# Quarter-block products of seven for the last two blocks' output matmul, with weight combinations made on GpSimd

## The chip, the cores and the metric

The kernel runs on one core of a Trainium2 chip. The metric is device time in microseconds (us) of one execution, the median of several. TensorE (PE in the profile, PEld its weight loads), VectorE (DVE), ScalarE (ACT), GpSimd (POOL) and SyncE (SP, which issues the DMAs here) run side by side and wait for one another through semaphores.

## The reference

Linear attention with exponential features feeds a feed-forward layer. There are 8 batches of 576 tokens with 8 heads of 64; side by side, the heads give 4608 tokens of 512 features.

```
phi(x) = concat(exp(p - m), exp(-(p - m)))     with p = x @ w_phi (64x128), m = max |p| of a token and head
kv = phi(k)^T v ; z = sum of phi(k) ; x = (phi(q) kv) / (phi(q) z + 1e-6)
h = x @ w_in                                   (4608x512 @ 512x2048)
g = h * erf(softplus(h))
out = g @ w_out                                (4608x2048 @ 2048x512), float32
```

## The kernel before

The feed-forward part works in nine blocks of 512 tokens (s = 0 to 8; blocks 0 to 7 are the first 512 tokens of each batch, block 8 the last 64 of all eight). A block's h is made in four units u of 512 features, each held as two tiles h of 128 x 1024. Numbers are split into two float16 parts, a rounded one and a remainder, and a product is three matmuls: high by high, high by low, low by high. Every matmul is issued as a pair, each of which fills 64 of the 128 output rows (`mm`).

x @ w_in is already made by seven products of quarter blocks instead of eight (the forms A11, S3, A12, S2, S1, S4, A22 of x against B11, T3, B21, T2, T1, B22, T4 of w_in; S and T are sums and differences of quarters). `split` makes the float16 parts of a form of x, which a DMA then transposes, and `combine` makes the sums; `split_weights` does both for w_in. For a unit, `h_unit` yields the seven products; `snap` (ACT) and `add` (DVE) take them out of the PSUM banks into h. `erf_gate` then runs softplus and erf on ACT and the multiplication by h on DVE, and splits g into `gh` (ACT) and `gl` (DVE).

g @ w_out is made plainly, by `o_piece`: for a half round (s, r, t), with r the half of the features and t the half of the tokens, four pieces of 12 matmul pairs of 512 columns. After r = 0 the sum goes to DRAM as a partial sum (`parts`), after r = 1 it is fetched, added to and stored.

The attention of the next batch runs between these on the same engines (`project`, `front`, `kv_piece`, `n_piece`, `t_piece`); it is done by about 760 us. The weights are loaded, unpacked and split between 18 and 258 us of the run.

The order of the work is set by a planner in the kernel (`Plan.run`). Every operation is recorded with an engine, an assumed cost, a priority and its buffers; the planner simulates the five engines with these costs and issues the operations in the order that it finds. So constants such as `STAY`, `SLACK` (how much later than planned an operand of TensorE is taken to be ready), `GATE_OFF` (priority offsets of the gate), the numbers of buffers and ranges such as `X_POOL` or `XC_POOL` (blocks whose work goes to POOL) move instructions on all engines. Operations marked `port=True` are assumed to exclude each other between DVE and POOL. Where TensorE would wait for over 600 ns by the plan, the planner issues filler matmuls on the tile `hot`, in pairs.

In `split_weights` four subtractions for each weight tile are recorded as work of POOL, but issued when `eng` already names DVE again:

```
    pool = u < T_POOL
    eng = nc.gpsimd if pool else nc.vector
    tt = lambda o, oc, x, xc, y, yc, r: op(POOL if pool else DVE, 750 if pool else 330, lambda: eng.tensor_tensor(...), ...)
    ...
    for f, x, c, key in (...):
        pool = u in LI_POOL and f in LF_POOL
        eng = nc.gpsimd if pool else nc.vector
```

## Time and profile before

| | us |
|---|---|
| median of 3 runs | 968.59 (968.54 to 968.77) |
| the profiled execution | 968.28 |
| its span, first to last instruction | 966.5 |
| TensorE busy | 947.7 |
| DVE busy | 752.7 |
| ACT busy | 681.9 |
| POOL busy | 43.9 |

Busy times are sums over the span and say little about a stage; the prediction reads them stage by stage. A row of a group gives the line of the kernel, the engine, the operation, the tiles written and read, and then count and durations; "idle before" is the time in which the engine waited, with what ended the wait. Matmul durations overlap, so their pace is read from the starts.

### The profile page before, as it was taken

Reading aid. Unit: us, or ns where it says so; the run is one execution under the profiler, and the core shown is the slowest. Engines: PE = TensorE matmul, PEld = TensorE weight load, DVE = VectorE, ACT = ScalarE, POOL = GpSimd, SP = SyncE. Lnnn points to the kernel's source line nnn. Section 1 sums busy time; section 2 is a strip of 40 time slices with the busy share of each in tenths; the row PEclk is TensorE's granted clock in tenths of the full one; section 3 lists DMA queues with packets and bytes.
Section 4 is the critical chain, followed back from the end, with each engine's and each line's share of the span. In section 5 each row is a group of like instructions: output and inputs, shape, how many; then the busy total and the mean of one; then the engine's idle time right before and its main releaser. Section 6 shows DMA issues by size and latency. Waiting matters only on the chain.

```text
span 966.5 us, 35295 instructions
## 1 busy us (share of the span) xinstructions
PE 947.7 (98%) x15806; PEld 754.5 (78%) x15806; DVE 752.7 (78%) x1351; ACT 681.9 (71%) x1000; POOL 43.9 (5%) x35
## 2 busy tenths in 40 slices
PE   9989989899999999999999999999999999999998
PEld 7878867768777878788787878787878787887875
DVE  6999999999977896898888886889896754335442
ACT  7877888777877576957687766766666755657571
POOL 0021100131310000000000000000000000000000
PEclk9999999999999999999999999999999999999999
DMA  9489999699855766386948493596735863342112
GB/s 330 113 217 307 271 283 289 240 324 304 175 164 159 186 123 205 84 212 148 224 120 196 127 221 101 142 223 166 164 69 148 219 153 132 110 144 89 56 56 77
DMA packets 173336, 170.82 MB, mean 177 GB/s; under 512 B 124544, under 2 KB 125696, under 8 KB 173184
## 3 DMA queue, kind: packets, MB, share of 16 engines
q1 hardware_dynamic: 173184, 168.57, 64.9%
q8 instruction: 123, 2.02, 0.9%
q14 instruction: 29, 0.24, 0.1%
HBM read 110.07 MB, written 29.10 MB: 144 GB/s over the span
## 4 chain that ended last, share of the span: by engine, by line
PE 78%; DVE 3%; issue 0%; DVEq 0%
PE bank L424 65%; PE bank L434 9%; PE bank L633 4%; DVE gl L1034 0%; DVE m L581 0%; DVE half L482 0%; DVE big L530 0%; DVE big L592 0%; DVE half L480 0%; DVE big L964 0%; DVE half L520 0%; DVE big L1030 0%; DVE uq L592 0%; DVE big L754 0%; DVE half L478 0%
## 5 line engine op out<-in xcount | busy, mean ns | idle before, releaser
L424 PE MATMUL bank<-half,big 128*64 128x256 f16 x4536 | 274.1, 273 | 3.4 <-DVE big L964 2.3
L424 PEld LDWEIGHTS <-big 128*64 128x64 f16 x4536 | 247.7, 110 | 22.8 <-issue 4.5
L442 ACT ACTIVATE big<-bank 128x512 f32<-128x512 f32 x190 | 111.1, 603 | 143.7 <-PE bank L424 140.5
L424 PE MATMUL bank<-woh,gh 128*64 128x512 f16 x1024 | 199.1, 380 | 2.3 <-ACT gh L1033 2.3
L424 PE MATMUL bank<-woh,gl 128*64 128x512 f16 x1024 | 198.6, 380 | 1.2 <-DVE gl L1034 1.2
L424 PE MATMUL bank<-wol,gh 128*64 128x512 f16 x1024 | 198.9, 379 | 0.0
L442 ACT ACTIVATE big<-big 128x512 f32<-128x512 f32 x206 | 127.6, 628 | 71.0 <-DVE big L592 35.0
L424 PEld LDWEIGHTS <-gh 128*64 128x64 f16 x2048 | 119.2, 110 | 74.7 <-ACT gh L1033 2.9
L964 DVE SCALAR_TENSOR_TENSOR big<-bank,big 128x512 f32<-128x512 f32 x108 | 73.9, 686 | 71.6 <-PE bank L424 67.0
L1030 DVE TENSOR_TENSOR big<-big,big 128x1024 f32<-128x1024 f32 x72 | 86.2, 1221 | 32.5 <-ACT big L1026 32.4
L581 DVE TENSOR_REDUCE m<-bank 128x4 f32<-128x512 f32 x144 | 92.7, 684 | 21.7 <-PE bank L633 21.5
L424 PEld LDWEIGHTS <-gl 128*64 128x64 f16 x1024 | 61.3, 110 | 45.9 <-DVE gl L1034 1.7
L424 PE MATMUL bank<-half,wi 128*64 128x256 f16 x1512 | 93.3, 273 | 1.2 <-DVE big L964 0.7
L1034 DVE TENSOR_TENSOR gl<-big,gh 128x1024 f16<-128x1024 f32 x64 | 80.4, 1265 | 13.5 <-ACT gh L1033 13.5
L424 PEld LDWEIGHTS <-wi 128*64 128x64 f16 x1512 | 81.4, 110 | 6.3 <-issue 1.9
L434 PE MATMUL bank<-kv,big 128*64 128x65 f32 x2304 | 84.6, 222 | 0.0
L434 PEld LDWEIGHTS bank<-v,big 128*64 128x64 f32 x2016 | 77.2, 137 | 8.0 <-ACT big L442 0.9
L434 PE MATMUL bank<-v,big 128*64 128x65 f32 (+1 forms) x2016 | 82.1, 228 | 0.3 <-ACT big L442 0.3
L434 PEld LDWEIGHTS bank<-kv,big 128*64 128x64 f32 x2304 | 78.6, 138 | 4.2 <-issue 0.2
L1010 ACT ACTIVATE big<-big 128x1024 f32<-128x1024 f32 x72 | 72.6, 1050 | 0.8 <-DVE big L964 0.4
L1033 ACT CAST gh<-big 128x1024 f16<-128x1024 f32 x64 | 65.5, 1039 | 4.0 <-DVE big L1030 3.9
L592 DVE TENSOR_TENSOR uq<-bank,m 128x512 f32<-128x512 f32 x72 | 49.2, 683 | 0.6 <-PE bank L664 0.5
(69 smaller groups left out, 1127.3 us busy)
## 6 DMA issues: line engine op xcount, KB each, us to landing
big<-wd SPq DMA_DIRECT2D x81, 512.0 KB, 5.0
ld<-in_qk_dram SPq DMA_DIRECT2D x31, 576.0 KB, 4.8
part<-half SPq DMA_DIRECT2D x36, 256.0 KB, 3.5
half<-part SPq DMA_DIRECT2D x36, 256.0 KB, 3.3
v<-in_vp_dram SPq DMA_DIRECT2D x28, 325.0 KB, 4.0
big<-in_moe_w_in_dram SPq DMA_DIRECT2D x32, 256.0 KB, 5.3
big<-in_moe_w_out_dram SPq DMA_DIRECT2D x16, 512.0 KB, 5.8
out_dram<-half SPq DMA_DIRECT2D x32, 256.0 KB, 2.3
```

The costliest lines, as they stand in the source:

```text
L424: nc.tensor.matmul(o[half], a[:, half], b, start=start, stop=stop, **kw)
L434: nc.tensor.matmul(o[half], a[:, half], b, start=first and c == 0, stop=last and c == 1)
L442: nc.scalar.activation(out_(), in_(), func, **k)
L581: op(DVE, 600, lambda: nc.vector.tensor_reduce(m.t, ps(), axis=AX.X, op=ALU.max, apply_absolute_value=True), r=[b], w=[m])
L592: op(DVE, 600, lambda: nc.vector.tensor_tensor(to(), ps(), m.t.unsqueeze(2).to_broadcast([P, GT, NF]), op=ALU.subtract), r=[b, m], w=[key])
L633: nc.tensor.matmul(both[nm].t[:, t * P : (t + 1) * P], x()[rows], w.t[rows, :], start=i == 0, stop=i == len(terms) - 1)
L964: op(DVE, 640, lambda: nc.vector.scalar_tensor_tensor(h.t[:, c * 512 : c * 512 + 512], b.t, HSCALE, h.t[:, c * 512 : c * 512 + 512], op0=A ...
L1010: fn = lambda: nc.scalar.activation(L.t, h.t, AF.Softplus, scale=1.0 / SG)
L1030: op(DVE, 1140, lambda h=h, L=L: nc.vector.tensor_tensor(h.t, h.t, L.t, op=ALU.mult), r=[L, h], w=[h], port=True, off=GATE_OFF[0] * (v + 1))
L1033: op(ACT, 940, lambda h=h, a=a: nc.scalar.copy(halfs(a), h.t), r=[h], w=[a], off=GATE_OFF[1] * (v + 1))
L1034: op(DVE, 1140, lambda h=h, a=a, b=b: nc.vector.tensor_tensor(halfs(b), h.t, halfs(a), op=ALU.subtract), r=[h, a], w=[b], port=True, off=G ...
```

## The change

For blocks 7 and 8 (`OW = 7`) g @ w_out is made by seven products too. `g_forms` takes the place of the two splits in `erf_gate`: for each unit four combinations of quarters of g on DVE, and seven splits, each a copy on ACT and a subtraction on DVE. `t_forms`, called once in each of the eight steps from step 16 on, makes the combinations of w_out on POOL out of the float16 parts held in `woh` and `wol`, splits them (ACT and POOL) and stores them to DRAM (`td`). `o_chunk` takes the place of `o_piece`: for each half of the features (r) 14 chunks of 12 matmul pairs of 256 columns, with the forms of g as weights and the forms of w_out as moving operand, and an addition in SBUF (`oc`) after each product instead of the partial sums in DRAM.

The diff changes more. The subtractions of `split_weights` now keep their engine (`eng=eng`), so they are issued on POOL. The remainders of x are made on POOL for all blocks and not for the first three alone, and the combinations of x on POOL for blocks 0 and 1. Seven copies of kv go from DVE to ACT, eight remainders of `halve` from POOL to DVE, and three more groups of keys take their maximum as a bias on ACT. Buffers that had sets of their own now share the 36 of `half`, and a dozen planner constants have other values.

```
-STAY2 = 9000.0
-N1 = 9
+STAY2 = 5000.0
+N1 = 5
-X_POOL = 0, 3
+X_POOL = (0, 9)
-XC_POOL = 0, 0
-HL_POOL = 8, 16
+XC_POOL = (0, 2)
+HL_POOL = (8, 12)
-HALF = 22
+HALF = 36
+N2 = 28
-W_EARLY = 4
+W_EARLY = 3
-BIASED = (0, 18)
-KV_ACT = (0, 0)
+BIASED = (0, 21)
+KV_ACT = (1, 8)
-GATE_OFF = (6000.0, 7000.0, 9000.0)
-W_FROM = 14
-W_EACH = 7
+GATE_OFF = (5000.0, 5500.0, 6500.0)
+W_FROM = 18
+W_EACH = 5
-STAY = 1500.0
+STAY = 4000.0
-SLACK = 2000.0
+SLACK = 1000.0
+OW = 7
+TW_FROM = 16
+TW_STEP = 1
+TW_POOL = 1
+T_AHEAD = 9000.0
...
-        tt = lambda o, oc, x, xc, y, yc, r: op(POOL if pool else DVE, 750 if pool else 330, lambda: eng.tensor_tensor(...
+        tt = lambda o, oc, x, xc, y, yc, r, eng=eng: op(POOL if pool else DVE, 640 if pool else 335, lambda: eng.tensor_tensor(...
...
+        if n[0] >= OW:
+            h0, h1 = hs.pop((n, 0)), hs.pop((n, 1))
+            for v, h in ((0, h0), (1, h1)):
+                L = pair[v]
+                op(DVE, 1140, lambda h=h, L=L: nc.vector.tensor_tensor(h.t, h.t, L.t, op=ALU.mult), ...)
+            g_forms(n, h0, h1, pair[0])
+            return
...
+    def g_forms(n, h0, h1, L):
...
+        def split_g(f, src, key):
+            g = gf[n, f] = buf("gf")
+            hv = lambda i: halfs(g)[:, i * 512 : i * 512 + 512]
+            act(520, lambda: hv(0), src, AF.Copy, [key], [(g, 0)], off=at[0])
+            op(DVE, 600, lambda: nc.vector.tensor_tensor(hv(1), src(), hv(0), op=ALU.subtract), ...)
...
+        split_g(A11, piece(h0, 0), (h0, 0))
+        mix_g(piece(L, 0), piece(h0, 0), piece(h1, 0), True, ...)
+        split_g(S3, piece(L, 0), L)
...
+    def t_forms(r, j):
...
+        for F in (4 * r + j, 8 + 4 * r + j):
+            want(("o", F))
+            f = buf("wf")
+            op(POOL_, k, lambda f=f, F=F: eng.tensor_tensor(f.t, woh.t[:, F, :], wol.t[:, F, :], op=ALU.add), ...)
...
+                act(310, lambda i=i, hv=hv: hv(i, 0), lambda x=x, c=c: x.t[:, c], AF.Copy, ...)
+                op(POOL_, k // 2 + 40, lambda ...: eng.tensor_tensor(hv(i, 1), x.t[:, c], hv(i, 0), op=ALU.subtract), ...)
+                op(SP, 430, lambda ...: nc.sync.dma_start(d.t[:, j * Q : j * Q + Q], o.t[:, i * Q : i * Q + Q]), ...)
...
+    def o_chunk(o, i):
...
+            for k in range(2):
+                for z, (gl_, wl_) in enumerate(((0, 0), (0, 1), (1, 0))):
+                    mm(109, lambda ...: (
+                        bank.t[:, k * Q : k * Q + Q], halfs(g)[:, gl_ * 512 + q * Q + k * P : ... + P], w(wl_)), ...)
...
+        if (s, key) not in outs:
+            c = outs[s, key] = buf("oc")
+            op(DVE, 600, lambda: nc.vector.tensor_scalar_mul(c.t, bank.t, scale), r=[bank], w=[c])
+        else:
+            c = outs[s, key]
+            op(DVE, 640, lambda: nc.vector.scalar_tensor_tensor(c.t, bank.t, scale, c.t, op0=ALU.mult, op1=ALU.add), ...)
...
+        plan.slack = SLACK if N2 > n > N0 else SLACK0
```

Two places show how the order moves. The first is the split of the first weight tiles of w_in, early in the program. DVE before: L520 are the subtractions in question, L480 and L482 unpack a weight tile, L530 makes its remainders, L581 and L592 belong to the attention.

```order
L520 TENSOR_TENSOR half11_153<-half0_142 128x256
L754 TENSOR_TENSOR big9_85<-bank3_64,dn0_195 128x4x64
L480 SCALAR_TENSOR_TENSOR half10_152<-big13_89,half10_152 128x512
L530 SCALAR_TENSOR_TENSOR wi00_73<-half0_142,wi00_73 128x256
L482 SCALAR_TENSOR_TENSOR half10_152<-big13_89,half10_152 128x512
L530 SCALAR_TENSOR_TENSOR wi00_73<-half11_153,wi00_73 128x256
L520 TENSOR_TENSOR half11_153<-half10_152,half0_142 128x256
L581 TENSOR_REDUCE m0_177<-bank4_65 128x4
L581 TENSOR_REDUCE m1_178<-bank1_62 128x4
L520 TENSOR_TENSOR half12_154<-half10_152,half11_153 128x256
```

DVE in the changed kernel at the same place (L505 was L482, L553 was L530, L607 was L581):

```order
L780 TENSOR_TENSOR big9_85<-bank3_64,dn0_203 128x4x64
L553 SCALAR_TENSOR_TENSOR wi00_73<-half12_162,wi00_73 128x256
L553 SCALAR_TENSOR_TENSOR wi00_73<-half15_165,wi00_73 128x256
L553 SCALAR_TENSOR_TENSOR wi00_73<-half17_167,wi00_73 128x256
L607 TENSOR_REDUCE m0_191<-bank4_65 128x4
L607 TENSOR_REDUCE m1_192<-bank1_62 128x4
```

And POOL in the changed kernel, where the four subtractions (L543) now stand, followed by a combination of x (L841) and remainders of x (L814):

```order
L543 TENSOR_TENSOR half17_167<-half12_162 128x256
L543 TENSOR_TENSOR half17_167<-half15_165,half12_162 128x256
L543 TENSOR_TENSOR half18_168<-half15_165,half17_167 128x256
L543 TENSOR_TENSOR half18_168<-half15_165,half18_168 128x256
L841 TENSOR_TENSOR half21_171<-big9_85 128x512
L814 TENSOR_TENSOR half22_172<-big9_85,half22_172 128x2x256
```

The four subtractions of a tile, eight times over, have left DVE, and POOL has them ahead of the forms of x.

The second place is the end of the program, after the last unit's softplus. ACT before, from the last erf on:

```order
L1026 ACT_TABLE_LOAD
L1026 ACTIVATE big9_85<-big9_85 128x1024
L1023 ACTIVATE big0_76<-big0_76 128x1024
L1024 ACT_TABLE_LOAD
L1033 CAST half11_153<-big5_81 128x1024
L1033 CAST half10_152<-big10_86 128x1024
```

ACT in the changed kernel from there on; the third copy behind the table load is the form A11 of the last unit, and the copies from big3 and big17 belong to the unit before:

```order
L1052 ACT_TABLE_LOAD
L1052 ACTIVATE big4_80<-big4_80 128x1024
L1049 ACTIVATE big8_84<-big8_84 128x1024
L1050 ACT_TABLE_LOAD
L465 ACTIVATE half28_178<-big3_79 128x512
L465 ACTIVATE half6_156<-big17_93 128x512
L465 ACTIVATE half0_150<-big1_77 128x512
L465 ACTIVATE half8_158<-big4_80 128x512
L465 ACTIVATE half1_151<-big1_77 128x512
```

TensorE in the changed kernel around the first use of that form (half0_150); the rows left out are the rest of the same 24 matmuls, of the 18 fillers, and of the next 24:

```order
L447 LDWEIGHTS half7_157
L447 MATMUL bank0_61<-woh0_74,half7_157 64x256
...
L1331 LDWEIGHTS hot_205
L1331 MATMUL bank2_63<-hot_205 64x512
...
L447 LDWEIGHTS half0_150
L447 MATMUL bank6_67<-woh0_74,half0_150 64x256
```

The two wide casts have become nine narrow copies, and 18 fillers stand ahead of the last unit's first out-product, where the order before had none. Between the last product of h and these fillers stand 152 matmuls of 256 columns. In the whole program the fillers number 98 instead of 90, and 14 of either stand at the very start.

167 lines of the change are left out of this document (138 added, 29 removed).

## The prediction

> **What bounds the kernel now.** I read the page's head, then a table of stretches, then the rows behind the stretches that differ.
>
> ```profile
> span 966.5 us, 35295 instructions
> PE 947.7 (98%) x15806; PEld 754.5 (78%) x15806; DVE 752.7 (78%) x1351; ACT 681.9 (71%) x1000; POOL 43.9 (5%) x35
> ```
>
> ```profile
> core 0: us, PE busy (x) PEld busy (x) DVE busy (x) ACT busy (x) POOL busy (x), PEclk, DMA share, GB/s
> 0.00:20.00 20.00, 18.55 (x290) 14.57 (x291) 11.99 (x25) 13.62 (x45) 0.70 (x6) 1.00 0.90 318
> 20.00:94.00 74.00, 69.45 (x1410) 59.72 (x1406) 72.87 (x190) 59.35 (x177) 10.47 (x9) 1.00 0.79 226
> 94.00:203.00 109.00, 101.05 (x1729) 82.69 (x1726) 107.02 (x213) 89.94 (x139) 19.11 (x12) 1.00 0.92 271
> 203.00:240.00 37.00, 37.00 (x624) 28.69 (x624) 36.58 (x62) 29.78 (x39) 2.56 (x2) 1.00 1.08 308
> 240.00:480.00 240.00, 240.00 (x4158) 186.79 (x4156) 204.22 (x346) 173.50 (x226) 11.09 (x7) 1.00 0.69 170
> 480.00:764.00 284.00, 283.62 (x5048) 224.79 (x5045) 231.75 (x417) 197.30 (x253) 0.00 (x0) 1.00 0.64 158
> 764.00:936.00 172.00, 172.00 (x2336) 140.57 (x2335) 79.19 (x94) 109.52 (x118) 0.00 (x0) 1.00 0.37 110
> 936.00:966.50 30.50, 26.05 (x242) 16.71 (x238) 9.13 (x11) 8.91 (x9) 0.00 (x0) 0.97 0.25 69
> ```
>
> Three stages. Up to 203 us DVE is the limit: it works 72.9 of 74 and 107.0 of 109 us, and TensorE is idle 1.45 + 4.55 + 7.95 = 13.95 us. From 203 us to the last matmul TensorE never pauses but for 0.38 us, at full clock, so there each microsecond of matmul taken away comes off the end. In the last stretch TensorE stops 4.45 us before the end, for the last addition and its store. Filler matmuls on the tile hot hide more idle time; after the first 14 they are 76, all before 90 us, in pairs as the ordinary ones:
>
> ```profile
> L1178 PE MATMUL bank<-hot x90: 376/379/636, 1.4 to 89.1; 128*64 128x512 f16 x90
> ```
>
> **The change, part by part.** *Fewer matmuls.* The pace stands in the rows of TensorE near the end, where the starts tell more than the modelled ends:
>
> ```profile
> 930.96 0.41 PE L424 MATMUL bank<-wol,half 128*64 128x512 f16 x2
> 931.17 0.63 PE L424 MATMUL bank<-woh,half 128*64 128x512 f16 x4
> 931.61 0.41 PE L424 MATMUL bank<-wol,half 128*64 128x512 f16 x2
> 931.82 0.63 PE L424 MATMUL bank<-woh,half 128*64 128x512 f16 x4
> 932.25 0.41 PE L424 MATMUL bank<-wol,half 128*64 128x512 f16 x2
> 932.47 0.63 PE L424 MATMUL bank<-woh,half 128*64 128x512 f16 x4
> 932.90 2.81 PE L424 MATMUL bank<-half,big 128*64 128x256 f16 x48
> 935.52 0.41 PE L424 MATMUL bank<-wol,half 128*64 128x512 f16 x2
> ```
>
> Three pairs of 512 columns start 0.648 us apart (930.96 to 931.61), 0.216 a pair; 24 pairs of 256 columns take 2.62 us (932.90 to 935.52), 0.109 a pair. Two blocks hold 2 x 16 x 12 = 384 pairs of 512 in o_piece, 82.9 us. Instead o_chunk makes 2 x 2 x 14 x 12 = 672 pairs of 256, 73.2 us. That is 9.7 us less, all in the stage where TensorE never waits. A pair of 256 columns loads as many weights as one of 512; the 0.109 us comes from h products that load at that rate too, so it already holds the loads.
>
> A rule of the Trainium skill speaks against this: TensorE: Matmul & The Clock Gate, section "Back-to-back issue gap", puts a stream of weight load and matmul at about 81 ns for 128 columns and 131 ns for 512, so that halving the columns saves far less than half. Interpolated, an estimate from that page, 256 columns would cost three quarters of 512. The trace disagrees: 0.109 is half of 0.216.
>
> *The start.* The diff also takes work from DVE before 240 us. In before the 32 subtractions of split_weights, meant for POOL, were issued on DVE (the name eng is bound again before they are issued); now they are on POOL. The 8 combinations of x of blocks 0 and 1 go to POOL too, 7 copies of kv and 3 subtractions to ACT, while 8 remainders of halve come back from POOL.
>
> ```profile
> L520 DVE TENSOR_TENSOR half<-half,half x24: 397/419/1118, 27.5 to 188.6; 128x256 f32<-128x256 f32 x24
> L520 DVE TENSOR_TENSOR half<-half x8: 396/421/425, 25.0 to 184.5; 128x256 f32<-128x256 f32 x8
> L1034 DVE TENSOR_TENSOR gl<-big,gh x12: 1209/1218/2175, 126.6 to 252.7; 128x1024 f16<-128x1024 f32 x12
> 186.16 1.01 DVE big L530 x3
> 187.50 1.20 DVE m L581 x2
> 192.34 5.37 POOL L788 TENSOR_TENSOR half<-big,half 128x512 f16<-128x512 f32 x1 [18.89 <-issue]
> 197.66 1.16 POOL L788 TENSOR_TENSOR half<-half,half 128x512 f16<-128x512 f32 x1
> 51.58 0.72 DVE L520 TENSOR_TENSOR half<-half,half 128x256 f32<-128x256 f32 x1
> 285.23 2.24 DVE L1034 TENSOR_TENSOR gl<-big,gh 128x1024 f16<-128x1024 f32 x1
> 228.15 0.66 DVE L964 SCALAR_TENSOR_TENSOR big<-bank,big 128x512 f32<-128x512 f32 x1
> ```
>
> On a full DVE an operation of 256 columns costs 0.33 us (1.01 for three), one of 512 costs 0.60. So the 32 subtractions are 10.6 us, the 8 combinations 4.8, kv copies some 2.3, the three subtractions 1.6: 19.3 us off. Back come 8 halves of halve, 5.4 in all, half of it this early. Counting the DVE rows of both orders up to the 18th addition of a product's bank (the one at 228.15 us) at these prices gives 207.7 us before and 194.6 after: 13.1 less, since some attention moves ahead too. That is the gain's upper end, close to the 13.95 us that TensorE idles. The lower end: POOL and DVE disturb each other. One POOL subtraction took 5.37 us instead of 1.16, and DVE operations that normally take 0.42 and 1.22 have maxima of 1.12 and 2.17. Thirteen DVE rows, the first at 51.58 us and the last at 285.23, stand 10.2 us above their medians, 0.35 for each of the 29 tensor operations of POOL up to then. Up to the last weight split POOL now has some 33 operations more, mostly short: up to 11.6 us given back, so a gain of 1.5; and none if TensorE then waits elsewhere. The order still holds 66 fillers after the first 14, against 76. I take the middle between 0 and 13.1, 6 us, since both prices are measured and the net lies between.
>
> By the Trainium skill (Perfetto Trace Analysis, section "Optimizing Scalar/DVE Operations") the two engines share a read port of SBUF, so that moving work between them might not help; by that this term is 0. The stretched rows agree that there is a conflict, not that it eats all.
>
> *The tail.* After the last product the old order has out-product pieces of earlier units to run. The new one has 76 pairs of 256, 8.3 us, then 9 filler pairs, then the first piece that needs the last unit. The latency comes from these rows:
>
> ```profile
> 935.06 1.28 ACT L1010 ACT_TABLE_LOAD   x1
> 936.35 2.00 ACT L1010 ACTIVATE big<-big 128x1024 f32<-128x1024 f32 x2
> 938.37 1.28 ACT L1026 ACT_TABLE_LOAD   x1
> 939.67 1.06 ACT L1026 ACTIVATE big<-big 128x1024 f32<-128x1024 f32 x1
> 940.63 1.04 ACT L1023 ACTIVATE big<-big 128x1024 f32<-128x1024 f32 x1
> 941.69 1.28 ACT L1024 ACT_TABLE_LOAD   x1
> 940.75 2.36 DVE L1030 TENSOR_TENSOR big<-big,big 128x1024 f32<-128x1024 f32 x2 [3.71 <-ACT big L1026]
> 943.03 0.69 DVE L1066 TENSOR_SCALAR half<-bank 128x512 f32<-128x512 f32 x1
> 962.08 0.69 DVE L1073 SCALAR_TENSOR_TENSOR half<-bank,half 128x512 f32<-128x512 f32 x1 [4.49 <-PE bank L424]
> ```
>
> Counted from the product's end (935.52), the last table load ends 7.45 us later. ACT then copies three quarters at about 0.6, the third being the one needed (9.25), and DVE subtracts (0.69): 9.9 us against 8.3 of cover. The fillers stretch this to 8.3 + 9 x 0.216 = 10.2, so the loss is 1.9 us. What follows is ready about as it is used. The last addition and store (4.45 us) stay.
>
> *What costs nothing.* Each of 8 units gets 7 splits and 4 combinations of 0.6 on DVE for two subtractions of 1.2: 4.2 us more, 34 in all, with 12 more additions 41; DVE works only 79 of 172 us from 764 on. ACT gets some 2 us more a unit, on 110 of 172. POOL's 80 forms of w_out and 42 remainders of x for blocks 3 to 8 lie behind 240 us; there DVE is busy 436 of 524 us, loses 42 x 0.6 = 25, and may be held 122 x 0.35 = 43. The stores and loads of the forms (4 and 8 MB), less 4 MB of partial sums, fall where the DMA share is 0.25 to 0.69. If this cover goes, TensorE waits at the first product of a block (below).
>
> *Order.* The planner's margin for TensorE (SLACK) falls from 2000 to 1000 ns, and to 600 from step 28. The trace shows no wait at the lower margin. It can gain no more than the 0.38 us idle after 203; at worst I allow 4, a third of what TensorE idles in the DVE-bound stage. I take 1, nearer to the full rows from 240 on.
>
> Sum: -9.7 - 6 + 1.9 + 1 = -12.8. The profiled execution took 968.28 us (span 966.5 and 1.8 around it), 0.3 below the median of 968.59: 955.5 against it, 956 as a median.
>
> **The rivals.** (a) The start gives nothing, because POOL holds DVE up for as long as it relieves it, and small waits come: -9.7 + 1.9 + 1 to 4 = 961.5 to 964.5. The 5.37 us row speaks for it; the short operations speak against. (b) The start gives all: -9.7 - 13.1 + 1.9 = 947.5. DVE's 98% up to 203 speaks for it; 66 fillers in the order against.
> (c) Slower: x remainders on POOL come late at the starts of blocks 3 to 8. SP issues in order, so a transpose waiting for POOL holds back the weight fetches behind it, and TensorE waits for either. Price: 5.37 - 1.16 = 4.2 us a block, six blocks 25 us: 968.3 - 12.8 + 25 = 981. It decides from the fourth late block on (12.8 / 4.2 = 3). Against it: blocks 0 to 2 had their remainders on POOL in the busiest stage, and no wait of TensorE there was put down to a transposed x. (d) The pieces of 256 columns cost three quarters of a 512: 672 x 0.162 = 108.9, 26 more than now, about 991 with the other terms (-6 + 1.9 + 1). The eight rows at 931 speak against it.
>
> **How the numbers follow.** My forecast, start term 2 to 11: 0.62. (a) 0.14, (b) 0.15, (c) 0.05, (d) 0.01; 0.03 for terms that cancel. A measurement here tells 0.2% (1.9 us). (a) and (b) are both faster, so faster 0.91, same 0.03, slower 0.06. The range leaves out the slow cases and the edges of (a) and (b): 948 to 964.
>
> **What would show it.** Right: matmuls of 256 columns on woh 0.109 a pair in blocks 7 and 8; 32 operations of L543 on POOL; TensorE idle before 203 us down from 13.95 to 6 to 10; 18 filler matmuls ending some 14 us before TensorE's end with no wait behind them over 0.3 us. Wrong: TensorE waiting between 240 and 764 us for a transposed x or for POOL, DVE rows stretched by more than 0.35 us for each POOL operation, or a hole at the tail well over 2 us.

## The result, and the profile after

The changed kernel takes 974.48 us (median of 4 runs, 973.05 to 976.77), the kernel before in the same comparison 968.68 (968.54 to 969.30): a ratio of 1.0062 (1.005 to 1.0074), 5.8 us slower. Forecast were 956.0 and 948 to 964. The profiled execution took 973.05 us, 4.8 more than that of before and the shortest of its four. The head of its page:

```profile
span 971.0 us, 36924 instructions
PE 944.2 (97%) x16390; PEld 783.3 (81%) x16390; DVE 801.7 (83%) x1354; ACT 713.1 (73%) x1097; POOL 210.0 (22%) x189
```

POOL works 210.0 us instead of 43.9, DVE 801.7 instead of 752.7, and TensorE is busy 3.5 us less. The table of stretches shows where TensorE's pauses are now (columns as in the prediction's table: the stretch, its length, busy time and count of PE, PEld, DVE, ACT and POOL, then the granted clock of TensorE, the DMA share and GB/s):

```profile
0.00:20.00 20.00, 18.55 (x296) 14.48 (x296) 11.90 (x25) 14.07 (x47) 0.70 (x6) 1.00 0.91 327
20.00:94.00 74.00, 69.10 (x1362) 58.16 (x1361) 72.76 (x173) 61.16 (x182) 29.97 (x30) 1.00 0.80 230
94.00:203.00 109.00, 103.39 (x1766) 83.43 (x1764) 107.64 (x190) 90.44 (x158) 32.54 (x26) 1.00 0.95 283
...
240.00:480.00 240.00, 233.97 (x4056) 186.88 (x4054) 208.36 (x319) 178.64 (x250) 101.00 (x96) 0.99 0.70 176
480.00:764.00 284.00, 282.59 (x5026) 226.31 (x5024) 229.82 (x394) 199.20 (x254) 33.79 (x24) 1.00 0.64 158
764.00:836.00 72.00, 69.68 (x918) 56.11 (x916) 40.59 (x53) 40.89 (x48) 9.45 (x7) 0.98 0.67 176
```

TensorE's idle time in a stretch is its length less PE's busy time. Up to 203 us it is 1.45 + 4.90 + 5.61 = 11.96 us, 2.0 less than before. From 203 to 836 us, where it was 0.38, it is now 6.03 + 1.41 + 2.32 = 9.76. The reader should also see two clocks that stood at 1.00 before: 0.99 and 0.98.

The rows of TensorE that carry most of the new pauses, the row behind one of them, and the pause of the tail; the bracket gives the wait and what ended it:

```profile
348.46 0.85 PE L659 MATMUL bank<-w,ld 64*128 64x128 f16 x24 [2.00 <-DVE big L780]
...
643.02 0.85 PE L659 MATMUL bank<-w,ld 64*128 64x128 f16 x24 [1.07 <-DVE big L618]
...
772.17 2.16 PE L447 MATMUL bank<-half,big 128*64 128x256 f16 x24 [2.32 <-DVE big L990]
774.06 1.55 PE L447 MATMUL bank<-woh,half 128*64 128x512 f16 x6
...
954.40 2.81 PE L447 MATMUL bank<-big,half 128*64 128x256 f16 x48 [0.46 <-DVE half L1171]
```

All of these waits are for DVE (of those over 1 us after 203 us one more, 1.10 at 277.71, is put down to ACT). At 348.46 and 643.02 the matmuls waiting are those of a projection (L659), at 772.17 those of a product of h. The last row is the pause of the tail. Two of the waits cost twice, as windows laid behind them show:

```profile
349.60:353.00 3.40, 3.40 (x30) 2.36 (x26) 3.30 (x7) 2.28 (x5) 0.00 (x0) 0.50 0.50 154
...
772.90:776.30 3.40, 3.40 (x27) 2.46 (x24) 2.38 (x4) 0.00 (x0) 0.00 (x0) 0.50 0.00 0
```

For 3.4 us after the wait of 2.00 and again after that of 2.32 the granted clock is 0.50. The 24 matmuls at 772.17 take 1.89 us from start to start of the next group (772.17 to 774.06), where 24 like them take 1.31 us in the tail rows below. Each of these windows costs some 1.7 us, half of its length.

What held DVE up ahead of 348.46 stands in its rows:

```profile
338.75 3.21 DVE L704 COPY half<-half 128x1024 uint16<-128x1024 uint16 x2
...
344.69 0.75 DVE L707 COPY big<-half 128x1024 uint16<-128x1024 uint16 x1 [2.13 <-DMA half<-half]
```

The copies of L704 prepare a transpose by DMA, and those of L707 take its result. The median of an L704 is 0.69 us; these two took 3.21 while POOL made combinations of w_out (L1111, 338.24 to 341.41). Then DVE stood 2.13 us until the transposed tile had landed, and the L780 that TensorE waited for came behind that.

And what held DVE up ahead of 772.17, with POOL's row in that time:

```profile
768.06 0.43 DVE L811 CAST half<-big 128x512 f16<-128x512 f32 x1 [2.35 <-DMA big<-tails]
768.40 0.68 DVE L841 TENSOR_TENSOR half<-big 128x512 f32<-128x512 f32 x1
769.00 2.18 DVE L1067 TENSOR_TENSOR half<-big,half 128x1024 f16<-128x1024 f32 x1
...
771.44 0.68 DVE L990 SCALAR_TENSOR_TENSOR big<-bank,big 128x512 f32<-128x512 f32 x1
...
768.62 1.48 POOL L814 TENSOR_TENSOR half<-big,half 128x512 f16<-128x512 f32 x1 [7.18 <-DVE half L811]
```

DVE works in the order of its rows. It waited 2.35 us for a load (tile tails), then made one of its subtractions (L1067) in 2.18 us, whose median over the run is 1.22, while POOL made a remainder of x (from 768.62 to 770.10). The addition that TensorE waited for (L990, 0.68 us) stood behind both. No form of w_out is in this, only the order and a remainder of x on POOL.

POOL's groups show what its operations really take (count, then busy time and mean ns of one):

```profile
L814 POOL TENSOR_TENSOR half<-big,half 128x512 f16<-128x512 f32 x54 | 79.0, 1470 | 426.8 <-DVE half L811 346.4 <-issue 46.1 <-ACT half L809 22.1
L1126 POOL TENSOR_TENSOR half<-half,half 128x256 f16<-128x256 f32 x32 | 25.6, 826 | 22.8 <-ACT half L465 22.8
L1116 POOL TENSOR_TENSOR half<-half,half 128x256 f32<-128x256 f32 x24 | 23.4, 985 | 0.6
L543 POOL TENSOR_TENSOR half<-half,half 128x256 f32<-128x256 f32 x24 | 22.8, 962 | 15.9 <-DVE half L505 13.1 <-DVE dn L766 2.2
L1111 POOL TENSOR_TENSOR half<-woh,wol 128x512 f32<-128x512 f16 x16 | 22.2, 1407 | 29.1 <-DVE half L704 29.1
```

The planner had been told 1160 ns for L814 and L1111, and 620 to 640 for L1116, L1126 and L543. Means are 1470, 1407, 985, 826 and 962. The rows of t_forms (L1111, L1116, L1126) lie at 220 to 388 us: their priority comes from steps 16 to 23, 500 us and later, but POOL was free, so the planner placed them far earlier. POOL is at work 101.0 of the 240 us between 240 and 480.

### The profile page after: what moved, and what is told of

It is laid out like the page before. It is cut to its first block, busy times and chain, and to the rows that moved or that the text cites. A ratio compares the mean times of both kernels' runs of the same rounds, so it can differ in the third digit from the quotient of the medians.

```text
span 971.0 us, 36924 instructions
## 1 busy us (share of the span) xinstructions
PE 944.2 (97%) x16390; PEld 783.3 (81%) x16390; DVE 801.7 (83%) x1354; ACT 713.1 (73%) x1097; POOL 210.0 (22%) x189
## 4 chain that ended last, share of the span: by engine, by line
PE 55%; DVE 28%; ACT 8%; DMA 5%; issue 4%; POOL 0%; SPq 0%; DVEq 0%; ACTq 0%; POOLq 0%
PE bank L447 44%; PE bank L457 7%; PE bank L659 3%; DVE m L607 3%; ACT big L465 2%; DVE half L1067 2%; DVE big L1063 2%; DVE big L553 2%; DMA half<-half 2%; DVE half L618 2%; DVE big L990 2%; ACT big L1036 2%; DVE half L505 2%; DVE half L503 1%; DVE ld L632 1%
## 5 line engine op out<-in xcount | busy, mean ns | idle before, releaser
L447 PE MATMUL bank<-woh,half 128*64 128x512 f16 (+1 forms) x2176 | 327.3, 362 | 2.0 <-DVE half L1067 0.8
L447 PEld LDWEIGHTS <-half 128*64 128x64 f16 x4032 | 231.8, 110 | 105.0 <-issue 4.8
L447 PE MATMUL bank<-half,big 128*64 128x256 f16 x4536 | 277.8, 274 | 2.3 <-DVE big L990 2.3
L447 PE MATMUL bank<-wol,half 128*64 128x512 f16 (+1 forms) x1088 | 204.3, 362 | 0.0
L465 ACT ACTIVATE big<-bank 128x512 f32<-128x512 f32 x190 | 111.1, 602 | 97.9 <-PE bank L447 88.9
L814 POOL TENSOR_TENSOR half<-big,half 128x512 f16<-128x512 f32 x54 | 79.0, 1470 | 426.8 <-DVE half L811 346.4
L465 ACT ACTIVATE big<-big 128x512 f32<-128x512 f32 x200 | 124.2, 628 | 56.1 <-DVE big L618 33.9
L607 DVE TENSOR_REDUCE m<-bank 128x4 f32<-128x512 f32 x144 | 92.5, 682 | 16.2 <-PE bank L659 15.7
L990 DVE SCALAR_TENSOR_TENSOR big<-bank,big 128x512 f32<-128x512 f32 x108 | 73.6, 684 | 31.5 <-ACT big L1036 19.6
L1063 DVE TENSOR_TENSOR big<-big,big 128x1024 f32<-128x1024 f32 x56 | 71.5, 1292 | 21.9 <-ACT big L1052 21.9
L1067 DVE TENSOR_TENSOR half<-big,half 128x1024 f16<-128x1024 f32 x56 | 74.5, 1340 | 6.5 <-ACT half L1066 6.1
L1066 ACT CAST half<-big 128x1024 f16<-128x1024 f32 x56 | 57.5, 1039 | 7.3 <-DVE big L1063 7.1
L707 DVE COPY big<-half 128x1024 uint16<-128x1024 uint16 x49 | 39.1, 804 | 20.9 <-DMA half<-half 20.9
L618 DVE TENSOR_TENSOR half<-bank,m 128x512 f32<-128x512 f32 x72 | 49.0, 681 | 0.2
```

The source lines that it names most:

```text
L447: nc.tensor.matmul(o[half], a[:, half], b, start=start, stop=stop, **kw)
L465: nc.scalar.activation(out_(), in_(), func, **k)
L607: op(DVE, 600, lambda: nc.vector.tensor_reduce(m.t, ps(), axis=AX.X, op=ALU.max, apply_absolute_value=True), r=[b], w=[m])
L618: op(DVE, 600, lambda: nc.vector.tensor_tensor(to(), ps(), m.t.unsqueeze(2).to_broadcast([P, GT, NF]), op=ALU.subtract), r=[b, m], w=[key])
L707: op(DVE, 640, lambda: nc.vector.tensor_copy(qview(qp)[:, 1, :].bitcast(U16).rearrange("p (n h) -> p h n", h=2), turned.t.bitcast(U16).rea ...
L814: op(POOL if pool else DVE, 1160 if pool else 600, lambda: eng.tensor_tensor(tv(1), view(), tv(0), op=ALU.subtract), r=[*reads, (t, 0)], w ...
```

## The experiments

One table first. "Against before" is the median less that of before in the same comparison (968.23 to 969.02), the ratio has its 95% interval, and TensorE's idle time is worked out from each kernel's own table of stretches, as above. Fillers are those outside the first 14, in pairs of 0.216 us; kernels with the seven products have 18 of them at the tail. The idle times and all rows of a kernel are those of its one profiled execution, which can lie off its median: that of e2_forms_dve by −2.6 us, of e7_slack2000 by −2.1, of e5b_before_consts_dve by +2.1, of e8_forms_spread by +2.2 and of e10_before_tt by +3.5.

| kernel | median (range, runs) | against before | ratio | idle to 203 | 203–480 | 480–836 | fillers |
|---|---|---|---|---|---|---|---|
| before (first profile) | 968.68 (968.54–969.30, 4) | | | 13.95 | 0.00 | 0.38 | 76 |
| changed | 974.48 (973.05–976.77, 4) | +5.8 | 1.0062 (1.005–1.0074) | 11.96 | 6.03 | 3.73 | 84 |
| e2_forms_dve | 966.18 (962.66–968.46, 10) | −2.1 | 0.9975 (0.9961–0.9989) | 11.07 | 2.17 | 3.48 | 84 |
| e1_forms_tiny | 969.80 (965.14–972.16, 10) | +1.6 | 1.0008 (0.999–1.0025) | 9.57 | 4.86 | 4.61 | 84 |
| e1b_no_act_wait | 970.49 (966.30–972.38, 7) | +2.3 | 1.0018 (1.0–1.0037) | 12.49 | 5.44 | 4.24 | 84 |
| e8_forms_spread | 970.78 (968.41–972.93, 10) | +2.1 | 1.0016 (1.0005–1.0028) | 12.16 | 3.80 | 7.89 | 84 |
| e3_true_costs | 973.07 (971.99–974.41, 4) | +4.4 | 1.0043 (1.0027–1.006) | 10.29 | 6.19 | 4.55 | 84 |
| e5_before_consts | 975.59 (973.76–977.64, 4) | +7.2 | 1.0076 (1.0055–1.0097) | 14.07 | 8.52 | 0.34 | 108 |
| e5b_before_consts_dve | 965.73 (964.43–969.81, 10) | −2.6 | 0.9978 (0.9967–0.999) | 11.54 | 2.32 | 1.38 | 108 |
| e6_xpool3 | 978.23 (973.39–979.61, 4) | +9.9 | 1.0094 (1.0066–1.0122) | 11.64 | 9.77 | 5.38 | 90 |
| e7_slack2000 | 970.82 (968.75–972.22, 8) | +2.5 | 1.0028 (1.0017–1.0039) | 11.77 | 6.41 | 3.14 | 84 |
| f1_dve_slack | 965.88 (965.20–967.65, 5) | −2.8 | 0.9971 (0.9958–0.9985) | 11.99 | 4.81 | 3.55 | 84 |
| e4_retune_only | 974.35 (973.59–976.66, 4) | +6.1 | 1.0068 (1.0053–1.0084) | 10.66 | 2.67 | 4.94 | 66 |
| g3_retune_no_pool | 978.23 (976.45–979.67, 4) | +9.6 | 1.0099 (1.0081–1.0116) | 13.57 | 2.88 | 4.50 | 86 |
| g4_retune_slack | 972.29 (971.62–973.31, 5) | +3.7 | 1.004 (1.0027–1.0053) | 9.83 | 3.06 | 3.08 | 66 |
| e10_before_tt | 969.28 (967.13–972.89, 10) | +0.6 | 1.0006 (0.9992–1.0021) | 9.27 | 4.37 | 0.17 | 94 |
| g1_seven_only | 966.25 (964.71–968.86, 7) | −2.4 | 0.9975 (0.9964–0.9986) | 13.77 | 4.26 | 0.00 | 94 |
| g2_seven_only_pool | 968.37 (967.12–969.52, 10) | −0.2 | 0.9996 (0.9986–1.0006) | 13.96 | 7.40 | 0.00 | 94 |
| g5_seven_late_dve | 963.16 (962.88–963.97, 5) | −5.9 | 0.9939 (0.9925–0.9953) | 12.96 | 0.78 | 1.11 | 94 |
| g6_seven_late_pool | 972.42 (970.40–973.72, 6) | +3.4 | 1.003 (1.0017–1.0043) | 13.26 | 0.19 | 8.05 | 106 |

### Who makes the forms of w_out

**On DVE instead of POOL.**

```
-TW_POOL = 1
+TW_POOL = 0
```

> TW_POOL = 0: the forms of w_out are made on DVE, planned anew. Theory P: DVE gets 16 x 0.6 + 80 x 0.33 = 36 us more work but no conflict there; DVE has 32 us to spare between 240 and 400 us and more behind, so the idle time between 240 and 480 us is 2 to 5 us and the time 967 to 973. Theory Q: as the changed kernel or worse, 973 or more.

Measured: 966.18, faster than before by 2.1 where the changed kernel is slower by 5.8: 7.9 us for the forms' place. (Such differences are made from the column "against before", since the comparisons ran on several chips.) The stretch that differs most:

```profile
240.00:480.00 240.00, 237.83 (x4128) 188.93 (x4124) 226.50 (x406) 179.72 (x252) 31.27 (x19) 1.00 0.72 179
```

TensorE's idle time between 240 and 480 us falls from 6.03 to 2.17, although DVE now works 226.5 us there instead of 208.4. That is 3.9 us. The two windows at half clock, 3.4 us, are missing too, but only in this execution, which took 963.56 us at a mean clock of 1.000: its wait of 2.14 us at 764.57, before the same addition of DVE (L990) as the one at 772.17, happened to be followed by full clock, while the ten runs of this kernel go down to a mean clock of 0.994 (the four of the changed kernel all show 0.996). So the rows account for about half of the 7.9. What stays is 3.48 us of idle time between 480 and 836, as much as in the changed kernel (3.73); its order brings that in any case (below). With the forms on DVE the whole order is planned anew, so this comparison holds the forms' place and a new order together; the next two kernels keep the order. (The expectation's 36 us count 80 short operations; there are 64 and 16 wide ones, about 31 us.)

**The same order, the POOL operations of t_forms only 8 columns wide** (the combinations of w_out are left out; the copies on ACT read woh, 512 columns of it instead of 256 of a form).

```
-eng.tensor_tensor(o.t[:, oc], x.t[:, xc], y.t[:, yc], op=ALU.subtract)
+eng.tensor_tensor(o.t[:, tiny(oc)], x.t[:, tiny(xc)], y.t[:, tiny(yc)], op=ALU.subtract)
```

> The order of all engines is that of the changed kernel; the operations of t_forms on POOL work on 8 columns instead of 256 or 512, and ScalarE's copies there read woh, so that they wait for nothing on POOL (the combinations of w_out are not computed). Theory P (the forms of w_out on POOL between 240 and 400 us hold DVE, ACT and SP up, and TensorE waits for these): TensorE's idle time between 240 and 480 us falls from 6.0 us to under 2, the window at half clock at 349 us goes, DVE's stretched rows there fall by most of 18 us, and the time falls from 974.5 to 965 to 968. Theory Q (it is the rest of the new order: lower margin for TensorE, remainders of x on POOL for all blocks): idle time there stays at 4 us or more, and the time stays above 971.

**The same order and POOL's work in full, but the copies on ACT read woh**, so that ACT waits for no form of POOL's (the high parts are then other numbers, and the remainders what is missing to the forms).

```
-act(310, lambda ...: hv(i, 0), lambda x=x, c=c: x.t[:, c], AF.Copy, [(x, c.start)], [(o, (i, 0))])
+act(310, lambda ...: hv(i, 0), lambda F=F: woh.t[:, F, 0:Q], AF.Copy, [(x, c.start)], [(o, (i, 0))])
```

> As the changed kernel, with all of t_forms' work on POOL, but ScalarE's copies there read woh instead of POOL's results, so ScalarE's queue does not wait for POOL (the high parts of the forms are not the right ones). If it is ScalarE's queue that hands the delay on (it waits 9.5 us for t_forms between 240 and 480 us): time as in the kernel with narrow forms, 965 to 968. If it is the conflict of POOL with DVE: gain under 2 us, 972 to 974.5.

Measured: 969.80 and 970.49, each between its two expectations. With the order kept, ACT's waiting for POOL is worth 3.5 us of the changed kernel's time, and that and POOL's time together 4.2; the 0.7 between them is not clear of noise (the intervals overlap), so that POOL's time costs anything by itself isn't shown by these two. The rest of the 7.9 came with the other order.

The narrow forms do take the stretch from DVE: the two copies of L704 ahead of the wait at 348.46 take 1.28 us instead of 3.21, and DVE works 197.8 us between 240 and 480 instead of 208.4. But the wait at that place is still there, and longer:

```profile
342.51 0.74 DVE L707 COPY big<-half 128x1024 uint16<-128x1024 uint16 x1 [6.28 <-DMA half<-half]
...
346.27 0.85 PE L659 MATMUL bank<-w,ld 64*128 64x128 f16 x24 [3.72 <-DVE big L780]
```

DVE was idle for 6.28 us before the transposed tile came. What made the transpose late isn't shown; in the profile the two issues of it on SP took 5.47 us, where the changed kernel's took 2.80. So a stretched DVE is not the only way to this wait; without any forms of w_out (e4_retune_only below) 0.78 us of it is left.

Two waits of the changed kernel bear on what else the forms hold up, first ACT's between 240 and 480 us, then those of SP's queue (the source line and tile waited for; us in total, times, longest):

```profile
ACT half L465 <- POOL half L1116: 9.5, 9, 4.7
```

```profile
SPq L1128 <- POOL half L1126: 13.8, 12, 5.1
```

ACT's copies in t_forms stand among its copies for the attention (also L465), so these wait along. The prediction had not named this. SP's stores of the forms (L1128) stand ahead of loads, but they wait as long with the forms on DVE (12.4 us in 10 waits), so they are not what makes POOL the dearer place.

**The same forms, spread over the blocks.** Each is held back in the plan until the unit has begun in whose step it is recorded.

```
-op(POOL_, k, lambda ...: eng.tensor_tensor(f.t, woh.t[:, F, :], wol.t[:, F, :], op=ALU.add), ...)
+plan.behind(op(POOL_, k, ...), first_evac[todo[15 + 4 * r + j]])
```

> The changed kernel, but the planner may start the forms of w_out on POOL only one weight-tile pair per step, from step 16 on, so they lie between about 500 and 690 us and not between 240 and 400 us. If it is the crowding (94 us of POOL in 160 us, beside a DVE that is busy 88%) that holds things up: idle time of TensorE between 240 and 480 us falls from 6.0 to 2.7 us or less, as in the kernel without seven products, little is added behind, and the time is 966 to 969. If POOL's forms cost the same wherever they stand: the idle time moves behind 480 us and the time stays at 972 to 975.

**The plan told nearly what POOL's forms take.**

```
-(POOL, nc.gpsimd, 1160)   k // 2 + 40
+(POOL, nc.gpsimd, 1400)   k // 2 + 250 (combinations), k // 2 + 130 (remainders)
```

> The changed kernel with the costs that the planner assumes for the forms of w_out on POOL raised to what the trace shows (1400 ns for a sum, 950 for a difference, 830 for a remainder, instead of 1160, 620, 620). If the waits come from a plan that is too short for POOL: idle time between 240 and 480 us under 3 us and 966 to 969. If from the conflict itself: 972 to 975.

Measured: 970.78, between its two expectations, and 973.07. Spreading gains 3.7 us, but in the profiled execution, the longest of ten, it moves the pauses rather than removing them: 2.95 us are left between 240 and 480 us, and 5.52 instead of 1.41 between 480 and 764. True costs in the plan give some 1.4 us (the intervals of the two ratios overlap), and TensorE still idles 6.19 us between 240 and 480 us. So most of the price is not the planner's ignorance of POOL's pace.

**Forms on POOL and on DVE under before's constants** (HALF and the new N2 apart), with the subtractions of split_weights on POOL in both:

```
-STAY2, N1, X_POOL, XC_POOL, HL_POOL, GATE_OFF, STAY, SLACK, ... as changed
+STAY2, N1, X_POOL, XC_POOL, HL_POOL, GATE_OFF, STAY, SLACK, ... as before
 TW_POOL = 1 in the first, 0 in the second
```

> The changed kernel's functions (seven products for blocks 7 and 8, forms of w_out on POOL, subtractions of split_weights on POOL) with the constants of the kernel before, but for the 36 shared buffers and the lower margin from step 28 on. Theory R (the loss is the other constants: the kernel with these alone measured 974.35): 968.2 - 9.7 matmuls + 1.9 fillers at the tail + 1.5 for 14 more fillers elsewhere + 2 to 4 for the forms on POOL = 964 to 966. Theory P (the forms on POOL by themselves): TensorE waits 6 us or more between 240 and 480 us and the time is 968 to 974.

> As the run before, with the forms of w_out on DVE. Theory R: 961 to 965, the two differing by 2 to 4 us. Theory P: 961 to 965 here and 968 or more there.

Measured: 975.59 and 965.73, both a little above their expectations. TensorE idles 8.52 us between 240 and 480 us with the forms on POOL and 2.32 with them on DVE. 9.9 us lie between the two, on another order: the price of the forms on POOL doesn't come from the changed kernel's constants.

### The x remainders: rival (c)

```
-X_POOL = (0, 9)
+X_POOL = (0, 3)
```

> The changed kernel with X_POOL = (0, 3): the remainders of x of blocks 3 to 8 are made on DVE again. If these on POOL cause the waits after 240 us: TensorE's idle time from 240 to 836 us falls from 9.8 us to 4 or less, 966 to 969. If not: 972 to 976.

Measured: 978.23, above both expectations and 4.1 us more than the changed kernel (the intervals of the two ratios just overlap). With the remainders of blocks 3 to 8 back on DVE, TensorE idles 9.77 us between 203 and 480 us and 5.38 after that. Rival (c) saw the slow end, but not its mechanism: remainders of x on POOL were no loss on this order.

### The order by itself

**The changed kernel without the seven products** (o_piece for all blocks, no t_forms).

```
-OW = 7
+OW = 9
```

> OW = 9: no block uses seven products for g times w_out and there are no forms of w_out; every other edit of the change stays. Theory P: the start's gain of some 4 us stays and nothing is lost between 240 and 480 us: 963 to 966, TensorE idle there under 1.5 us. Theory Q: TensorE still waits 4 us or more between 240 and 480 us; 970 or more, since the 9.7 us of matmuls come back.

Measured: 974.35, as much as the changed kernel.

```profile
240.00:480.00 240.00, 237.33 (x4130) 191.63 (x4126) 198.10 (x327) 170.20 (x221) 31.75 (x19) 1.00 0.69 165
480.00:764.00 284.00, 281.96 (x5014) 228.71 (x5010) 225.26 (x388) 197.80 (x251) 31.55 (x22) 1.00 0.64 156
764.00:836.00 72.00, 69.10 (x944) 56.41 (x940) 36.02 (x44) 42.04 (x45) 9.45 (x7) 1.00 0.55 154
```

No forms are made here, and still TensorE idles 2.67 + 2.04 + 2.90 us where the kernel before paused for 0.38 in all. The moves of work, the shared buffers and the new constants cost 6.1 us by themselves. The wait of 2.90 us is the one before the addition L990, at 768.00. Against this kernel the seven products with forms on DVE are worth 974.35 − 966.18 = 8.2 us, near the 7.3 of the prediction's two terms and the tail's pause (9.7 − 1.9 − 0.5).

**The margin back at 2000 ns**, in the changed kernel, with forms on DVE, and without the seven products:

```
-SLACK = 1000.0
+SLACK = 2000.0
```

> The changed kernel with SLACK = 2000 instead of 1000 for steps 7 to 27. If the lower margin causes the waits after 240 us: idle time from 240 to 836 us falls from 9.8 us to under 3, no window at half clock, 962 to 967. If not: 971 to 976.

> Forms of w_out on DVE and SLACK = 2000: if the two edits, worth 8.3 and 3.7 us each by itself, act on different waits: 961 to 963.5. If on the same: 965 to 967.

> The changed kernel without the seven products, the POOL moves kept, and the margin for TensorE's operands back at 2000 ns. Theory (POOL moves): stays within 2 us of 974.4, the reordering with the smaller margin. Rival (the margin): falls to 968 to 970, and TensorE's idle time after 240 us from 7.6 us to under 2.

Measured: 970.82 (3.3 less than the changed kernel), 965.88 (0.7 less than with forms on DVE alone, with intervals that overlap) and 972.29 (2.4 less than without the seven products, between the two expectations). The first lies just below the range in which the margin would not matter: TensorE's idle time from 203 to 836 us is 9.55 us, hardly less than 9.76, so the expectation that the margin makes these waits is not met, and in the profiled execution, the shortest of eight at a mean clock of 1.000, only the windows at half clock are gone. With forms on POOL and without the products the margin pays; with the forms on DVE there is little left for it to win.

**The constants alone**, with the subtractions, the x remainders, the combinations of x and halve on the engines that they had before, and no seven products:

```
-X_POOL = (0, 9)   XC_POOL = (0, 2)   HL_POOL = (8, 12)   eng=eng
+X_POOL = (0, 3)   XC_POOL = (0, 0)   HL_POOL = (8, 16)
 OW = 9
```

> The changed kernel without the seven products and without the moves to POOL (subtractions of split_weights on DVE, x remainders on POOL for blocks 0 to 2 alone, combinations of x on DVE, halve as before): the planner's constants alone. Theory (the +6 of the reordering without seven products come from the work put on POOL): 967 to 970. Rival (they come from the constants, the smaller margin above all): 973 to 976.

Measured: 978.23, the rival's side and beyond its number. On these constants the work put on POOL is a gain of some 3.5 us (9.6 − 6.1; the intervals just touch); what costs is in the rest, the constants above all. The copies of kv and the biases that went to ACT and the shared buffers are in this kernel too. With the work on POOL in place the margin is 2.4 of the 6.1. Which of the others carries the rest wasn't tried.

### The subtractions of split_weights on POOL

Before, with this alone:

```
-tt = lambda o, oc, x, xc, y, yc, r: op(POOL if pool else DVE, 750 if pool else 330, ...
+tt = lambda o, oc, x, xc, y, yc, r, eng=eng: op(POOL if pool else DVE, 640 if pool else 335, ...
```

> The kernel before with the subtractions of split_weights really issued on POOL, alone. The prediction's step on the start (DVE relieved by 10.6 us, up to half given back): TensorE idle before 203 us under 10 us, 962 to 966. Rival: what POOL takes from DVE and 9 more filler pairs eat it: 967 to 972.

Measured: 969.28, no difference from before (0.9992 to 1.0021).

```profile
203.00:240.00 37.00, 34.92 (x622) 28.51 (x620) 33.81 (x58) 29.10 (x40) 3.00 (x2) 1.00 1.09 315
240.00:480.00 240.00, 237.71 (x4120) 186.55 (x4116) 202.41 (x341) 172.83 (x223) 9.50 (x7) 1.00 0.67 165
```

Idle time up to 203 us falls from 13.95 to 9.27. But the plan sets 18 more fillers (9 pairs, 1.9 us), and 2.08 and 2.29 us of idle time come after 203 us where there were none: 4.7 gained, 6.3 given back. That is in an execution of 972.79 us; in the median the two cancel.

### The seven products by themselves

Before with the seven products added, nothing else moved; forms on DVE, then on POOL.

```
 kernel before
+OW = 7, g_forms, t_forms, o_chunk, the shared buffers, N2 = 28
+TW_POOL = 0 in the first, 1 in the second
```

> The kernel before, its constants and its division of the other work between the engines, with the seven products for blocks 7 and 8 added; the forms of w_out are made on DVE, the subtractions of split_weights stay on DVE. Theory (the matmul term of the prediction holds, -9.7 and +1.9 at the tail, and what is missing in the kernel with the subtractions on POOL is the price of moving them): 960 to 963, TensorE idle before 203 us near 14 as before, under 4 after it. Rival (the seven products themselves bring about 3 us of waits and fillers with them, whoever makes the subtractions): 964.5 to 967, as measured with the subtractions on POOL.

> The same with the forms of w_out on POOL: the change of the title alone, on the order of before. Theory (the forms on POOL cost 8 to 10 us wherever they stand): 8 to 10 above the kernel with the forms on DVE in this call, TensorE idle 6 to 9 us between 240 and 480 us. Rival (the price comes only together with the other work that the change puts on POOL, the subtractions and the x remainders): within 3 us of the kernel with the forms on DVE.

Measured: 966.25 and 968.37. Both are their rivals' numbers. Left to themselves the seven products save 2.4 us and not the 7.8 of matmuls and tail fillers (9.7 − 1.9). Of the missing 5.4, 4.3 us stand in one stretch, and in it in two rows of TensorE:

```profile
240.00:480.00 240.00, 235.74 (x4110) 186.17 (x4106) 228.68 (x421) 181.71 (x255) 10.84 (x7) 1.00 0.72 185
```

```profile
347.45 0.85 PE L659 MATMUL bank<-w,ld 64*128 64x128 f16 x24 [2.08 <-DVE big L780]
388.81 0.85 PE L659 MATMUL bank<-w,ld 64*128 64x128 f16 x24 [2.09 <-DVE big L618]
```

Both are projections (L659) waiting for DVE, which the forms raise from 204.2 to 228.7 busy us in this stretch. The forms on POOL cost 2.1 us more than that, less than on the other two orders (7.9 and 9.9). But that the price needs POOL's other new work doesn't follow, as the last experiment shows: between 240 and 480 us both places are bad, and POOL the worse.

### The forms later

```
-TW_FROM = 16
+TW_FROM = 20
-op(POOL_, k, lambda ...: eng.tensor_tensor(f.t, woh.t[:, F, :], wol.t[:, F, :], op=ALU.add), ...)
+plan.behind(op(POOL_, k, ...), first_evac[todo[19 + 4 * r + j]])
 forms on DVE in the first kernel, on POOL in the second
```

> The seven products on the order of before, forms of w_out on DVE, but held back in the plan until units 19 to 26 are under way (about 600 to 770 us) instead of 260 to 390 us. Theory (what the seven products lose are the two waits between 240 and 480 us behind a DVE that the forms fill up): TensorE idle there from 4.26 us to under 1, and 962 to 964.5. Rival (the waits move with the forms, as they did when the changed kernel's forms were spread): 965.5 to 967, the idle time between 480 and 836 us instead.

> The same with the forms on POOL, held back alike. The plan puts 6 more filler pairs (1.3 us) in. Theory (crowding on POOL and the conflict with a full DVE between 240 and 480 us are the price, and POOL is empty later): 963.5 to 966. Rival (the waits move): 967.5 to 969.5.

The forms on DVE now lie between 568 and 770 us, where they lay between 260 and 405.

Measured: 963.16 with the forms on DVE, 5.9 us faster than before and 11.7 than the changed kernel; 972.42 with the same forms on POOL, above both expectations, with no other new work on POOL. The price of POOL is 9.3 us here, 1.3 of it 6 more pairs of fillers. The first one's table of stretches:

```profile
240.00:480.00 240.00, 239.50 (x4150) 187.91 (x4148) 203.34 (x344) 173.04 (x226) 10.99 (x7) 1.00 0.68 169
480.00:764.00 284.00, 282.89 (x5030) 224.85 (x5028) 257.23 (x488) 206.12 (x280) 0.00 (x0) 1.00 0.69 169
```

DVE's work has moved from the stretch where it made TensorE wait (203.3 us, as before) to the next one (257.2 of 284), and TensorE idles 0.50 and 1.11 us. The two waits of 2.1 us were the price, and the place was their cause. On POOL the same holding back did the reverse: from 0.2 us below the kernel before to 3.4 above it.

What goes wrong there with the forms on POOL is seen where a new block begins. DVE with the forms on DVE, and DVE with the forms on POOL, at the same work (L811 and L814 split the forms of x, L841 combines them, L780 is what a projection waits for):

```profile
628.91 0.68 DVE L841 TENSOR_TENSOR half<-big 128x512 f32<-128x512 f32 x1
629.51 0.68 DVE L814 TENSOR_TENSOR half<-big,half 128x512 f16<-128x512 f32 x1
630.11 0.42 DVE L811 CAST half<-half 128x512 f16<-128x512 f32 x1
...
630.58 0.68 DVE L814 TENSOR_TENSOR half<-half,half 128x512 f16<-128x512 f32 x1
...
631.53 0.42 DVE L780 TENSOR_TENSOR big<-bank,dn 128x256 f32<-128x256 f32 x1
```

```profile
628.49 0.42 DVE L780 TENSOR_TENSOR big<-bank,dn 128x256 f32<-128x256 f32 x1
...
630.00 1.36 DVE L811 CAST half<-big 128x512 f16<-128x512 f32 x1
631.29 1.22 DVE L841 TENSOR_TENSOR half<-big 128x512 f32<-128x512 f32 x1
632.42 1.21 DVE L814 TENSOR_TENSOR half<-big,half 128x512 f16<-128x512 f32 x1
633.56 0.94 DVE L811 CAST half<-half 128x512 f16<-128x512 f32 x1
...
634.79 0.84 DVE L814 TENSOR_TENSOR half<-half,half 128x512 f16<-128x512 f32 x1
635.66 0.42 DVE L780 TENSOR_TENSOR big<-bank,dn 128x256 f32<-128x256 f32 x1
```

POOL in the second kernel in that time:

```profile
628.34 2.74 POOL L1111 TENSOR_TENSOR half<-woh,wol 128x512 f32<-128x512 f16 x2 [0.74 <-DVE dn L764]
...
631.92 3.16 POOL L1116 TENSOR_TENSOR half<-half,half 128x256 f32<-128x256 f32 x3
```

L811, L841 and L814 take 0.42, 0.68 and 0.68 us in the first kernel. While POOL makes its forms they take 1.36, 1.22 and 1.21, then 0.94 and 0.84. L780 stands behind them, and TensorE waits for it:

```profile
636.13 1.28 PE L659 MATMUL bank<-w,ld 64*128 64x128 f16 x24 [3.52 <-DVE big L780]
```

These five rows lose 2.7 us in all; the wait is 3.52 us, and the 24 matmuls behind it take 1.28 us instead of 0.85, at a granted clock of 0.57 between 636 and 640 us. By the Trainium skill (GPSIMD Engine Reference, section "8. Key points") GpSimd and VectorE contend where a VectorE instruction reads two SBUF inputs or runs in a two-port mode. The trace agrees as far as it goes: L780, which reads a PSUM bank, took its usual 0.42 us at 628.49, beside POOL's L1111.

## Why the prediction was wrong, by its own steps

**Fewer matmuls, −9.7: right.** The pace in the changed kernel, and the fillers of the tail:

```profile
946.57 1.50 PE L447 MATMUL bank<-big,half 128*64 128x256 f16 x24
947.88 0.30 PE L447 MATMUL bank<-woh,half 128*64 128x256 f16 x2
...
949.18 2.14 PE L1331 MATMUL bank<-hot 128*64 128x512 f16 x18
```

24 matmuls are 12 pairs: 946.57 to 947.88 is 1.31 us, 0.109 a pair, half of the 0.216 of 512 columns. Rival (d), the pace of three quarters, is refuted: on this kernel 256 columns cost half. With the forms out of the way (the last kernel with DVE) the sum is −9.7, +1.9 for the tail's fillers, +0.5 for its pause, +1.5 of pauses from 203 to 836 us and −1.0 at the start, −6.8. With one window at half clock behind the wait at 136.85 us (+1.7) that is −5.1, as much as lies between the two profiled executions (963.16 and 968.28); the medians differ by −5.9.

**The tail, +1.9: right.** The 18 fillers stand from 949.18 to 951.13, 1.95 us, and end some 15 us before TensorE does. The pause behind them is 0.46 us; the limit named was 0.3.

**The start, −6: wrong by half, and worth nothing alone.** In the changed kernel idle time up to 203 us fell by 2.0, to 11.96 and not to 6 to 10, and the fillers there by 5 pairs, 1.1 us. The subtractions alone gave 969.28 against 968.68. The step that failed took the middle between 0 and 13.1 because "both prices are measured". What stood against it in the forecast was the better guide: rival (a), the start gives nothing. For the subtractions alone the term is 0, as by the Trainium skill's sentence that the prediction cites on the shared port (Perfetto Trace Analysis, section "Optimizing Scalar/DVE Operations"). That the port is the reason isn't shown: the idle time up to 203 us did fall, by 4.7, and came back as fillers and later waits.

**"What costs nothing": wrong, 2 to 10 us by the order, 7.9 on the changed kernel's.** With the order below it is one of the two steps that turned the sign. It gave POOL's 80 forms the room "behind 240 us" and DVE 43 us of holding up, and found that both fit. They fit as sums: between 240 and 480 us the narrow forms free DVE of only 10.5 us. But the forms ran within 170 us, POOL's operations took 826 to 1407 ns where the plan had 620 to 1160, and what counted was not DVE's sum but which rows stood between a stretched or late operation and the operand that TensorE needed next. The rows at 348, 636 and 772 us show this; ACT's waiting for POOL, worth 3.5 us with the order kept, the prediction had put at nothing without a reason. The text had named the consequence ("If this cover goes, TensorE waits at the first product of a block") and gave it no chance and no price; its only slow rival with POOL was the x remainders, which do no harm: back on DVE they made the kernel slower. How much of the 7.9 is POOL's conflict with DVE and how much the other order that the planner finds stays open.

**Order, +1, between −0.38 and 4: wrong, 6 to 10 us.** Reordering alone costs 6.1 us, the constants alone 9.6. The term was bounded by the rows of the old order, in which TensorE was full from 203 us on; it says nothing of how near that order was to pausing, nor of what another order does. Which of the constants costs it stays open.

Laid against the profiled executions, in us: matmuls −9.7, start −2.0 and −1.1, tail +1.9 and +0.5, idle time from 203 to 836 us +9.4, two windows at half clock +3.4. That is +2.4 of the +4.5 between the spans; 2 us are not placed by these rows. By experiments the way to +5.8 is +6.1 (the reordering), −8.2 (the seven products, forms on DVE), +7.9 (the forms to POOL); these add up by construction, each being the step from one kernel to the next.

## What to carry to other kernels

Work that is needed late should be tried later, where the engine beside the critical one has room: the same instructions on VectorE were 3.5 us dearer at 260 to 405 us than at 568 to 770. It is no rule: on GpSimd the later place was 3.6 us the dearer. An idle GpSimd is not always a free place for element-wise work while VectorE feeds TensorE (the remainders of x gained there, the forms of w_out lost on each of four orders); count the rows ahead of the next operand that it will stretch, not its share of busy time. And when a change rewrites the planner's constants along with the mathematics, price the order as a change of its own.

## What the runs showed of the hardware

TensorE's clock was halved for about 3.4 us after waits of 2.00 and 2.32 us in the changed kernel, and was at 0.57 for 4 us after the wait of 3.52 in the last. Waits of 2.08 and 2.09 us in the kernel with the seven products alone, of 2.14 with the forms on DVE and of 2.90 in the reordering alone were followed by full clock. One and the same wait, 2.02 us at 136.8, was followed by full clock in the kernel before (1.00 from 136 to 142 us) and by 0.57 in the kernel with the forms late on DVE (136.8 to 140.2). The Trainium skill (TensorE: Matmul & The Clock Gate, section "Part 1: The HAM clock gate") speaks of an idle window of some 3.4 us; here waits of 2.0 were enough at times. This makes the time of one kernel vary: with the narrow forms the ten runs go from 965.14 us at a mean clock of 1.000 to 972.16 at 0.991; with the forms late on DVE, which leave no wait over 1.4 us after 203 us, five runs lie within 1.1 us.

POOL's subtraction of 256 columns takes 0.67 to 0.79 us in the median of the changed kernel (L1126, L543), but 0.83 and 0.96 in the mean, with single ones up to 1.80: GpSimd's operations are stretched at times too, not only VectorE's.
